# All loop matmuls in 64x64 parts of the array, in two phases of 64 rows into PSUM bank pairs

## The chip, the cores and the metric

The kernel runs on one core of a Trainium2 chip. A core has a matrix engine (TensorE, "PE" in the profile; its weight loads stand apart as "PEld"), two engines that can read the matrix engine's results (VectorE, "DVE", and ScalarE, "ACT"), GpSimd ("POOL") and SyncE ("SP"), which here mostly issue DMAs. Results of matmuls land in PSUM: 8 banks of 128 partitions by 512 fp32 values. The metric is device time in microseconds. The kernel before took 957.39 us, the median of three runs (953.36, 957.39 and 957.76).

A weight load puts up to 128 rows by 128 columns of weights into the array, and a matmul streams N columns of data past them. The array can be used whole (128*128 in the profile's forms), as two halves of 64 rows (64*128), or as four parts of 64 rows by 64 columns (64*64), each of which has weights, data and results of its own. The profile's form `64*64 64x512` is a matmul in one such part with 512 columns of data. Four of them, one in each part, do the work of one whole matmul; this text calls them a foursome.

## The reference

The inputs are u and v (8 batches of 3136 rows by 256), z (8 by 3136 by 64), three weight matrices and a filter. What is computed, per batch:

```python
scores = np.matmul(z, z.transpose(0, 2, 1)) / S        # S = 3136
attn = np.maximum(scores, 0.0) ** 2
x = u * np.matmul(attn, v)
x1, x2, x3 = split(x @ w_proj, 3)                      # 256 columns each
x2_conv = irfft(rfft(x2, axis=1) * rfft(filter, axis=0), n=S, axis=1)
out = (x1 * x2_conv * x3) @ w_out
```

The matrices of the attention are far too large to be stored, so scores are made in pieces, squared, and summed into the product with v at once. The Fourier transforms are matmuls with cosines and sines in two steps (64 by 49), with a trip through DRAM between the steps.

## The kernel before, in words

**Tiling.** The 3136 columns of a batch are cut into 7 chunks (five of 512, one of 256, one of 320: `CHUNKS`, L18), and its rows into 25 tiles of 128 (the last has 64). For each batch and chunk the kernel goes through a list of units of two tiles (four for the chunk of 256).

- **Scores** (letter S, `score_mm`, L1692): a unit's scores go into a PSUM pair, two banks, one for each tile. The contraction is over 64 values only, so the two tiles run in the two halves of the array. ACT or DVE makes R, the positive part (`relu`, L1929, lines L1934 and L1936), and then A, its square (`sq`, L1938, lines L1943 and L1945). Scores are symmetric, so some units aren't computed but taken from an earlier chunk's A by a DMA transpose (tiles `M1`, `M2e`, `M2o`).
- **Weighing** (letters W, w and v, `weigh` L1753 and `weigh_rows` L1736): A times v is summed over all units of the chunk into two accumulators of one bank each, `ps_o0` and `ps_o1` (L577), one for each half of the 256 model columns. A W does this with whole 128*128 matmuls (line L571 in the profile, the helper `matmul`). A w with its later v does the same in halves: first the upper 64 rows into one accumulator and the lower 64 rows into the other, and then, in v, the other way round. [...] This text calls such a change a flip.
- At a chunk's end DVE multiplies the accumulators by u into `xT` (`xe`, L1980, line L1989), which frees them for the next chunk.
- **Projections and first transform** (letters A, and Z in the last batch; `add_proj` L1195, `dft1` L1004): x1, x2 and x3 of the chunk, each in several tasks with one PSUM bank, evicted by ACT or DVE 512 columns at a time (`copy`, L604 and L608), and for x3 by the product with x1 (`gate`, L1231). x2 goes through the first transform and to DRAM (`spec`).
- **Spectrum** (letter Q, `add_quads` L1150): second transform, product with the filter's spectrum (L1323 to L1328), and its inverse. These matmuls run in 64*64 parts and use a PSUM pair, whose banks are evicted by two instructions.
- **End** (letter B, `add_end` L1391): the last transform in matmuls of 128 columns (weights `conv_in`, data `T4`), the gate (L1420), the product with w_out (weights `yT`, data `wo`), and the store.

**PSUM.** Three pairs (`ps_t`, L531) serve S, Q and, bank by bank, A, B and Z; the other two banks are the accumulators.

**What sets the order.** The order of all PE work is a string, `ORDER` (L47): each letter takes the next task of its kind. A second string, `ENGINES`, says of each task that ACT or DVE could do which of them does it. The class `Plan` (L245) walks the string with modelled costs to place everything else in time. In the loop `go` (L381) a change between whole matmuls (A, B, Z, W) and matmuls in halves or parts (S, Q, w, v) is charged 0.096 us, and a flip is held back for `TURN` (0.235 us) after the earlier rows' end:

```python
            if self.mode and half != (self.mode == "S"):
                start += 0.096
...
                elif self.flip not in (None, task.flip):
                    start = max(start, self.turned + TURN)
```

When a stretch of letters S, Q, w, v holds a Q, all its matmuls use 64*64 parts, otherwise 64*128 halves (`plan.quarters`).

Of the kernel before, what the change touches and what calls it, by code (L numbers as in the profile page):

```python
# [11 lines left out]
P = 128  # L12
F32 = mybir.dt.float32
# [5 lines left out]
N1 = 64  # L19
# [16 lines left out]
SPARE = 0.25  # L36
# [3 lines left out]
MOST = 6  # L40
TURN = 0.235
REACH = 2
# [5 lines left out]
    "ASSAWSSAWWSSAWwSwSvvSSwWBWSSvSWWSSSWWWWWWSSSWWWWwwSvSwwvSSvSwwwSvSvvvAAAWWWABABAWWWAWWAWAAAAAAWBSSww"  # L48
    "SvSSvwwwSvvSwvSSvWWBWWBWWWBWWBWAAAAWWSwSSwwwSSvvvSwwSvvvSWAWAWABAWWWBWWWAWSwSSwWWASwSSvvvSSSWWWWAAWB"
    "WWWASSWAAAWWBWAWWASwSSvwSSvSWWWBSSWAAWWAAAWAWBWWBwSwSwSSwwSvvvvvSWBWWWAAWWAWAAAWWSSSWWWwSvSSWAAWSSwS"  # L50
    "wwQQvvvSQSWWWWSSAAWWWAWAAAWWAAAAWSSwSwwSQvwvvQSvwSQwSwSWAAvvQSvSWWWWWSQSWWWWAwSwSvvSwwQSSvwwQvSvwvSS"
    "vWAWAWWAWAWAWAAWWAAWAQQwQwSSwwAAAAQvvQwvvSwSSvwSvQvSWWAWWWSQSWWAWAWWSQwSwwSvwQvSvwQSwQvvSvSWWWWWAAWW"
    "WAWAWWAQSWAAAAWSwSSwQvQvSWWAWWWSSSWAAWAAAWWAWSSwSwwwSvSvvwvSvSSWAWWAAWAAWWSSSWWWWBBAWBWWBWAAWSSSwwSv"
    "vSSWWABBBWWBAAAAAWWBBWWASSAWWWASSBWBAAAWSwSwSvvwSvwSwwSvSSvvWAWBBWBAWWWBAWWBAWAWSSwwSwSSWABABvSvQvwS"
    "SwSvwvSSvQWWWWBWWAWSAWAWAWQQwSwQvwvSwQwSvvvwSSvwQvSWWBBAAAAWSQSWWBBWWAAWAAWWABQQWwSSQvwSwwQvSwQvvSSv"
    "WWAWABWAWWSQSWWAAWWWAAWAAAAAWSSwQwQvSvSWAASWWWWWSSSWWWWwSwwSwSSvwwvSvvSvvSWWWWBWAWWSSWBWWWABBAWBASww"
    "SSvwSvwSSvvSwwBABAWBBASvSvSWWBWAWAABABWWWABAAAWWSwSSWBAWBAvwSwwSSvwSvvSvSWWBABBWAWBAAAWWAAWBWWSSSWWA"
    "AAAABSwSwwSQvvQvwSSwwQvvSvQSWWWWBWWWASQAWWWQSSwwwSWAWvSQwQvvwSSvBWAABAWSSvQWWWSSQWWWAWWwQQwwSwQvvSSv"
    "vwSSWWWWSvSWBAWAWWWWAAWABAAWASwwSQwwSSvvvSQvWWBAWAABWAWWQSSWWWAAWAWwSSSwwwSSvvAAWvSvSSWWWAWWWSSWWAAB"
    "WBBAWABAWBABSwSwSwwSvvSvwwSvwSSvvvSAWWWAABABBBWABWWSSBBWAAAWABWBWAAAWSSwwSwSvwwvvSSvvwSSvABBWWWWSSSW"  # L60
    "WWAAAWBAWAABAWSSQwWBBWBASvSSwwSwSQvwvvQvQSWWWWAWWAAWWBAWABWSQwQwwSwSvvSQSvvwQwQvQvSWAWBWAAAWWWAWAWSS"
    "SWWWAWBQQwwSQvwvSSwSwvwQSvvQvSWWWWWAWAWAAWWAWQwwSSvvSwwSSvSvWWWAWAAAWAWAAAWWWWSSwSvSwwSSvABAAwSvSwwS"
    "vvvSSWAWBWBWBWWBWBWSSAWBWWASSwSvwSSWABWBAAAwSvSSvwwSvSvWBWWABWAWWAAABAAWAAAWSSSWWAWWWBBwSSvwSvwSSSvW"
    "WWWWBAWBASSWAWBBAWWWSwwSwSvvSSvwSwwSvSvvwQvSSWWWWABWAWAAWAWWWWQQSwwQSvwwvQSSvwvwQQvSvWBWWAABAAAABBWW"
    "WSSWAAWWQQSWBWSwwSQwQvSwvSQvwSWAWvvSSWWAWWAWAAWAWWWASwQvwQwSvSwvSSvWAWWAAWWWAAWAWWWSSQwwwSSvwwvSSvQv"
    "vSSBWAWBASSBWWWAAAWAAWWSSSWWWBAWwSSwSWWBASvSvwwSSvwvSSvBWABAWABBBAAAAWAABAWBWWSSSWWABWBWWABSwSSwwwSw"
    "SvvSvvSSvWWBABWSSAWBWBWABWAWAAAWWAAABWSwSwwSvSvvSwwwQSvQvSvwQWWBBvQSAAWBWWWWWAWABAAAAWQwwwSSSvvvQwww"
    "SQvSvwSvSvSWAAWWBWWSSQWWWBAWAWWSQQwwwSwQQvvvSwvSwQvSvSWAWAWAWWBWAWAWSQAWWWAWSSwwQSWvvSQSWWWWBWAWAAWA"
    "AWWSwSSvwSvSwwSvvSSWWWBAAWWAAWWBWWSSSWWBBBAAWBBWSwSvSwwSSvBWABBAWSwSSvvwSvSABWWBWWSSSWWBWABAAWWBBAWA"
    "AABAABWAASwSSvwwSwSvwvSwSvSvvSSWWWWWBWAWAWABWWSSwQwwwSSvvQwvSwvSQvvwQSvQWBWBAWABWWWAAWWAQSWWBAwSwQQv"  # L70
    "wSwQvwwSwSQvvvQvvSQSWWWWAWWAWWBAAWAWSwSwSSvvSwwwSvvSSvSWWWWAWBWAWWQSSWWWWWAWASSwQwQvvSABAWWWBWBWWWWS"
    "QWWSSwwSSvwvSSvWWWZWWWWWWWAZZAAZAAZAZBZZBZBZBZBZBZBZBBZBZZQQQZQQQQQQQQQZQQQQBBZBZZZZZZBZZZZZBZZZBZBZ"
    "BZBZBBZBBBBBBBBBBBBBBBBBBBBBBB"
)
# [2008 lines left out]
```

## Time and profile before

| what | value |
|---|---|
| times of three runs | 953.36, 957.39, 957.76 us |
| span of the profiled execution | 958.1 us |
| PE busy | 923.5 us, 96% of the span, 9264 matmuls |
| weight loads busy | 508.8 us, 53%, 9352 loads |
| DVE busy | 861.3 us, 90% |
| ACT busy | 836.5 us, 87% |
| POOL busy | 198.1 us, 21% |
| mean granted TensorE clock | 0.989 |

The profiled execution has 958.1 us from its first to its last instruction, 0.7 us more than the median of the timed runs, so sums made against its span are carried over to the time by taking off 0.7 us. A line of groups gives engine, operation, result and operands by the program's names, the form (weights' rows * columns, then data's partitions x elements), the count, and after the bar the busy time with the mean duration of one; after the second bar stands the engine's idle time before them. A row of the timeline gives start, length, engine, and how many instructions of one kind are merged in it. A matmul's end is modelled: a matmul of 512 columns is drawn some 380 ns long although the next one starts earlier than that. So the pitch, from start to start, says more than the drawn lengths, and a gap in the issue that is shorter than the drawn tail doesn't show as idle time.

### The profile page before, as it was taken

Reading aid. Unit: us, or ns where it says so; the run is one execution under the profiler, and the core shown is the slowest. Engines: PE = TensorE matmul, PEld = TensorE weight load, DVE = VectorE, ACT = ScalarE, POOL = GpSimd, SP = SyncE. Lnnn points to the kernel's source line nnn. Section 1 sums busy time; section 2 is a strip of 40 time slices with the busy share of each in tenths; the row PEclk is TensorE's granted clock in tenths of the full one; section 3 lists DMA queues with packets and bytes.
Section 4 is the critical chain, followed back from the end, with each engine's and each line's share of the span. In section 5 each row is a group of like instructions: output and inputs, shape, how many; then the busy total and the mean of one; then the engine's idle time right before and its main releaser. Section 6 shows DMA issues by size and latency. Waiting matters only on the chain.

```text
span 958.1 us, 24530 instructions
## 1 busy us (share of the span) xinstructions
PE 923.5 (96%) x9264; PEld 508.8 (53%) x9352; DVE 861.3 (90%) x1508; ACT 836.5 (87%) x1145; POOL 198.1 (21%) x426
## 2 busy tenths in 40 slices
PE   7999899999999999999999999999999999999986
PEld 3444555455455655546555565555555465565654
DVE  8886789898899997999899998899999989999896
ACT  6977699998889998998989989899988999998674
POOL 5132311122112111213031121121211320101031
PEclk8999999999999999999999999999999999999989
DMA  9999889967999789997999979998799989885768
GB/s 147 167 150 171 133 154 186 195 132 152 193 207 194 151 172 178 200 196 146 174 212 203 172 162 177 186 195 167 169 176 210 198 155 194 183 204 126 188 186 264
DMA packets 332423, 170.64 MB, mean 178 GB/s; under 512 B 242598, under 2 KB 307942, under 8 KB 332304
## 3 DMA queue, kind: packets, MB, share of 16 engines
q1 hardware_dynamic: 302424, 132.28, 67.3%
q0 software_dynamic: 29168, 35.13, 24.8%
q10 hardware_dynamic: 712, 1.66, 0.6%
q8 instruction: 73, 1.20, 0.5%
q14 instruction: 46, 0.38, 0.2%
HBM read 90.26 MB, written 53.35 MB: 150 GB/s over the span
## 4 chain that ended last, share of the span: by engine, by line
PE 85%; DMA 6%; DVE 3%; issue 2%; ACT 2%; SPq 2%; POOL 0%; DVEq 0%; ACTq 0%; POOLq 0%
PE ps_s L571 35%; PE ps_o_t L571 27%; PE ps_o_t L1734 23%; DMA spec_in_t<-spec 1%; DMA M_t<-spec_in_t 1%; DMA conv_in_t<-spec 1%; ACT R_t L1934 1%; DMA A_t<-spec 1%; DMA M2e_t<-A_t 1%; DMA spec<-gs_t 0%; DVE xh L1323 0%; DMA M_t<-A_t 0%; SPq L1048 0%; DMA spec<-uT_t 0%; DVE R_t L1936 0%
## 5 line engine op out<-in xcount | busy, mean ns | idle before, releaser
L1934 ACT ACTIVATE R_t<-ps_s 128x1024 f32<-128x1024 f32 (+2 forms) x349 | 325.2, 973 | 34.5 <-PE ps_s L571 29.0
L1943 ACT ACTIVATE A_t<-R_t 128x1024 bf16<-128x1024 f32 (+3 forms) x307 | 304.5, 1018 | 13.7 <-DMA M2e_t<-A_t 6.0
L571 PE MATMUL ps_o_t<-A_t,v_t 128*128 128x512 bf16 (+2 forms) x1080 | 250.2, 352 | 6.0 <-issue 5.1
L1734 PE MATMUL ps_o_t<-A_t,v_t 64*64 64x512 bf16 (+5 forms) x2708 | 228.3, 355 | 0.1
L1945 DVE TENSOR_TENSOR A_t<-R_t 128x1024 bf16<-128x1024 f32 (+4 forms) x185 | 197.3, 1087 | 13.4 <-ACT R_t L1934 11.6
L571 PEld LDWEIGHTS <-v_t 128*128 128x128 bf16 x1534 | 139.5, 98 | 129.6 <-issue 31.9
L1936 DVE TENSOR_SCALAR R_t<-ps_s 128x1024 f32<-128x1024 f32 (+4 forms) x163 | 178.1, 1110 | 23.5 <-PE ps_s L571 13.0
L1734 PEld LDWEIGHTS <-v_t 64*64 64x64 bf16 (+1 forms) x3808 | 134.1, 103 | 106.9 <-PE ps_o_t L1734 21.4
L571 PE MATMUL ps_s<-zT_t 64*64 64x512 bf16 (+4 forms) x1521 | 175.6, 352 | 7.6 <-ACT R_t L1934 4.2
L654 POOL COPY tick<-xT_t 1x1 bf16<-1x1 bf16 x54 | 11.6, 214 | 648.0 <-DVE xT_t L1989 648.0
L571 PE MATMUL ps_s<-xT_t,wp 128*128 128x512 bf16 (+2 forms) x412 | 108.2, 353 | 2.0 <-DVE yT_t L1420 0.4
L604 ACT ACTIVATE x_t<-ps_s 128x512 bf16<-128x512 f32 (+2 forms) x149 | 82.5, 579 | 29.1 <-PE ps_s L571 25.7
L571 PEld LDWEIGHTS <-zT_t 64*64 64x64 bf16 (+1 forms) x1554 | 64.1, 102 | 76.1 <-issue 40.3
L1989 DVE SCALAR_TENSOR_TENSOR xT_t<-ps_o_t,uT_t 128x256 bf16<-128x256 f32 (+2 forms) x224 | 75.8, 380 | 12.6 <-PE ps_o_t L571 9.4
L1231 DVE TENSOR_TENSOR gate_t<-ps_s,x_t 128x256 bf16<-128x256 f32 (+2 forms) x220 | 74.2, 382 | 11.1 <-PE ps_s L571 8.5
L1323 DVE TENSOR_TENSOR xh<-xh,H 128x1024 bf16<-128x1024 bf16 x120 | 81.4, 682 | 0.6
L1734 PE MATMUL ps_o_t<-M_t,v_t 64*64 64x512 bf16 (+2 forms) x808 | 65.6, 364 | 0.0
L1420 DVE TENSOR_TENSOR yT_t<-ps_s,gate_t 128x512 bf16<-128x512 f32 (+2 forms) x99 | 59.0, 618 | 5.6 <-PE ps_s L571 4.6
L645 POOL DMA_DIRECT2D un_t<-in_u_dram x112 | 60.1, 559 | 6.1 <-issue 2.5
L664 POOL DMA_DIRECT2D v_t<-in_v_dram x112 | 59.1, 549 | 10.6 <-issue 6.1
L571 PEld LDWEIGHTS <-wp 128*128 128x128 bf16 x448 | 42.4, 98 | 33.9 <-issue 5.3
L571 PE MATMUL ps_s<-wp,xT_t 128*128 128x256 bf16 x400 | 58.8, 273 | 0.1
(175 smaller groups left out, 1029.2 us busy)
## 6 DMA issues: line engine op xcount, KB each, us to landing
out_dram<-ost_t SPq DMA_DIRECT2D x60, 256.0 KB
spec<-s_t SPq DMA_DIRECT2D x96, 128.0 KB
spec_in_t<-spec SPq DMA_DIRECT2D x56, 192.0 KB
spec<-gs_t SPq DMA_DIRECT2D x56, 192.0 KB
v_t<-in_v_dram POOLq DMA_DIRECT2D x80, 128.0 KB, 5.1
un_t<-in_u_dram POOLq DMA_DIRECT2D x80, 128.0 KB, 5.6
conv_in_t<-spec SPq DMA_DIRECT2D x34, 256.0 KB
out_dram<-ost_t SPq DMA_DIRECT2D x18, 128.0 KB
```

The costliest lines, as they stand in the source:

```text
L571: wrote(nc.tensor.matmul(o, *args, **kw), o)
L604: got = nc.scalar.activation(out_, in_, AF.Copy)
L645: nc.gpsimd.dma_start(out=t[ds(j * N1, N1), lo - t0 : hi - t0, :], in_=x[:, n2 : n2 + hi - lo, :])
L664: nc.gpsimd.dma_start(out=t[ds(j * N1, N1), ds(v_at(a), (b - a) * D)], in_=r[:, n2 + a - lo : n2 + b - lo, :].rearrange("p t d -> p (t d)"),)
L1231: got = nc.vector.tensor_tensor(g[:, ::-1] if h == 0 else g, p, x, ALU.mult)
L1323: nc.vector.tensor_tensor(x[:, 1 - i], x[:, 0], h, ALU.mult)
L1734: row_sums[dh] = h, nc.tensor.matmul(*args, **kw)
L1934: has_read(nc.scalar.activation(r, p, AF.Relu), p)
L1936: has_read(nc.vector.tensor_single_scalar(r, p, 0.0, ALU.max), p)
L1943: nc.scalar.activation(a, r, AF.Square)
L1945: (nc.vector if e == "DVE" else nc.gpsimd).tensor_tensor(a, r, r, ALU.mult)
L1989: nc.vector.scalar_tensor_tensor(x, f, inv_s2, ut, ALU.mult, ALU.mult)
```

## The change

- Every matmul of the loops now runs in 64*64 parts. The form of the array is a property of the task (`full`): only the transposes of the setup (four for z, one for T4, two for TZ) are still whole.
- The letter W is gone. All 648 weighing tasks of the string are now w, each with its v.
- Tasks of A, B and Z are made by `two`: a first phase, in which the upper 64 rows feed bank 0 of a pair and the lower rows bank 1, and a second phase, a letter of its own later in the string, with the rows swapped. Ahead of the second phase PE waits for the first one's last matmul.
- PSUM is four pairs for everything. The accumulators of a chunk are one pair, taken from the four when the chunk's first w starts, and freed by the eviction. A task that used one bank now takes a pair, and what were two evictions of 512 columns is one of 1024 (`dft1`, x1, x2, Q outside the last batch, the gates, `xe`, the end); the tiles in SBUF are joined to fit.
- The square of R now carries the scale 1/S, so that `xe` is a plain product.
- One projection task covers the chunk where x2, the first transform and the output product had one task for each two tiles.
- Both strings are new. `ORDER` has 2637 letters (648 w, 648 v, 512 S, 424 A, 229 B, 136 Q, 40 Z) where it had 2530 (643 W, 285 w, 285 v, 512 S, 408 A, 222 B, 136 Q, 39 Z); `ENGINES` has 1426 (921 for ACT, 505 for DVE) where it had 1746 (1137 and 609).

The core of the diff:

```diff
-MOST = 6
+FORM = 0.096
...
 ORDER = (
-    "ASSAWSSAWWSSAWwSwSvvSSwWBWSSvSWWSSSWWWWWWSSSWWWWwwSvSwwvSSvSwwwSvSvvvAAAWWWABABAWWWAWWAWAAAAAAWBSSww"
+    "ASSASwSAvSwAvSwSvwSwSvvwSwSvSvwSvwSvwSvwSvwBvwSvSwAvAwSwSvwwvSSwwAvvSwvSwwvAvvvwBvBwSwwSSvwAAAAvwvSv"
...
-            if self.mode and half != (self.mode == "S"):
-                start += 0.096
-                self.flip, self.parted = None, True
...
+            if self.full is not None and self.full != task.full:
+                start += FORM
+            self.full = task.full
+            if k in "wv":
+                flip, turned = self.flips.get(task.sum, (0, 0.0))
+                if k == "w":
+                    task.flip = flip
+                    task.second.flip = flip ^ 1
                     self.rest.append(task.second)
-                elif self.flip not in (None, task.flip):
-                    start = max(start, self.turned + TURN)
-                self.flip, self.parted, self.turned = task.flip, False, start + task.cost["PE"]
+                elif flip != task.flip:
+                    start = max(start, turned + TURN)
+                self.flips[task.sum] = task.flip, start + task.cost["PE"]
...
-    ps_t = [ps_p.tile([P, 2, 512], F32, name=f"ps_s{i}") for i in range(3)]
+    ps_t = [ps_p.tile([P, 2, 512], F32, name=f"ps_s{i}") for i in range(4)]
...
-    banks = Banks(3)
-    pair_slots, one_slots, half_slots = Pairs(banks), Singles(banks), Halves(banks)
-    ps_o = [Pool(f"ps_o{dh}", 1, [P, 512], F32, PS) for dh in range(2)]
+    pair_slots = plan.pairs = Pairs(4)
...
+    def two(kind, mm, cost, deps=(), takes=(), **kw):
+        box = {}
+
+        def go(ph):
+            if ph == 0:
+                box["p"] = take_pair()
+            else:
+                rest = nc.tensor.nop()
+                for x in box["last"].values():
+                    tc.add_manual_dep(
+                        rest.ins, x.ins.name, mybir.DependencyInfo(needs, reason.DATA),
+                        reason="the other rows' sum",
+                    )
...
+        a = pe(kind, lambda: go(0), cost, deps, [pair_slots, *takes], **kw)
+        b = pe(kind, lambda: go(1), cost, [(a, TURN - LAT["PE"])], **kw)
+        return a, b, box
+
+    QUARTERS = [(h, c) for h in range(2) for c in range(2)]
...
-            for m in range(0, P, N1 if plan.quarters else P):
-                n = N1 if plan.quarters else P
-                matmul(o[ds(m, n)], zt[h, ds(t * P + m, n)], zt[h, ds(C0[at], cw)], start=True, stop=True)
+            for m in range(0, P, N1):
+                matmul(o[ds(m, N1)], zt[h, ds(t * P + m, N1)], zt[h, ds(C0[at], cw)], start=True, stop=True)
...
+    def weigh(un, flip, ph):
 
         b, c, k = un
         cw = CHUNKS[c]
+        if k == 0 and ph == 0:
+            acc[b, c] = take_pair()
+        todo = [(i, t) for i, t in enumerate(plans[b, c][k][1]) if t < NT - 1]
+        for i, t in todo:
+            for m in range(0, P, N1):
                 for h in range(2):
                     dh, at = h ^ flip, slice(h * N1, (h + 1) * N1)
                     by_rows(
+                        (b, c, dh), h, laid(un, acc[b, c][ds(m, N1), dh, :cw]), row(v16[b], t)[at, ds(dh * P + m, N1)], block(un, i, at),
+                        start=k == 0 and i == 0 and ph == 0, stop=k == len(plans[b, c]) - 1 and ph == 1 and i == todo[-1][0],
                     )
...
-                    nc.scalar.activation(a, r, AF.Square)
+                    nc.scalar.activation(a, r, AF.Square, scale=1.0 / float(S))
                 else:
-                    (nc.vector if e == "DVE" else nc.gpsimd).tensor_tensor(a, r, r, ALU.mult)
+                    nc.vector.scalar_tensor_tensor(a, r, inv_s2, r, ALU.mult, ALU.mult)
...
+                    for h, n in halves(c):
+                        x, f = by_half(xt["t"][:], h, n), by_half(acc[b, c][:], h, n)
+                        ut = uT[b, c][:, 0:n, :, ds(h * N1, N1)].rearrange("p t d j -> p d t j")
+                        has_read(nc.vector.tensor_tensor(x[:, :, ::-1] if h == 0 else x, f, ut, ALU.mult), f)
```

More of the change, by code (lines that the diff above doesn't have):

```diff
@@ L39 @@
 ZP, ZL = 0, 0.0
-MOST = 6
+SPARE = 0.25
 TURN = 0.235
+FORM = 0.096
 REACH = 2
@@ L232, in __init__ @@
         self.clogs = False
-        self.second, self.split, self.flips, self.flip = None, False, False, None
+        self.second, self.flips, self.flip, self.full, self.sum = None, (), 0, False, None
         for d, _ in self.deps:
@@ L1754, in weigh, with add_weigh @@
+    w_first, w_last = {}, {}
+    def add_weigh(un, data, done):
         b, c, k = un
[L1755 to L1770 removed]
```

732 lines of the change are left out of this document (317 added, 415 removed).

## The prediction

> **What bounds the kernel now.** I read the page first: the engines' shares and the chain of waits.
>
> ```profile
> span 958.1 us, 24530 instructions
> PE 923.5 (96%) x9264; PEld 508.8 (53%) x9352; DVE 861.3 (90%) x1508; ACT 836.5 (87%) x1145; POOL 198.1 (21%) x426
> ...
> PE 85%; DMA 6%; DVE 3%; issue 2%; ACT 2%; SPq 2%; POOL 0%; DVEq 0%; ACTq 0%; POOLq 0%
> ```
>
> PE is busy 96% of the span and holds 85% of the chain, with DVE and ACT close behind at 90% and 87%. Next I asked for busy times by stretch, to see whether that holds everywhere.
>
> ```profile
> 100.00:900.00 800.00, 786.66 (x8216) 438.71 (x8294) 734.80 (x1255) 725.83 (x985) 151.10 (x325) 1.00 0.92 177
> 900.00:958.00 58.00, 44.75 (x454) 29.60 (x454) 45.76 (x95) 31.97 (x62) 12.28 (x23) 0.91 0.76 226
> ```
>
> The columns are PE, PEld, DVE, ACT and POOL, then clock, DMA share and GB/s. From 100 to 900 us PE idles 13.3 of 800 us at full clock; only the last 58 us, with 13.2 us idle, are of another kind. So the middle is worth what PE's own instruction stream is worth, and "busy" has to be looked into, since a drawn tail can cover a gap in the issue. Third, then, the timeline of PE alone:
>
> ```profile
> 402.17 0.41 PE L571 MATMUL ps_s<-zT_t 64*64 64x512 bf16 x4
> 402.41 0.39 PE L571 MATMUL ps_s<-xh,TZ 64*64 64x512 bf16 x4
> 402.72 0.61 PE L571 MATMUL ps_s<-wp,xT_t 128*128 128x256 bf16 x4
> 403.17 1.46 PE L571 MATMUL ps_o_t<-M2o_t,v_t 128*128 128x512 bf16 x6
> 404.56 0.41 PE L571 MATMUL ps_s<-spec_in_t,S 49*64 49x512 bf16 x4
> 404.80 0.39 PE L571 MATMUL ps_s<-zT_t 64*64 64x512 bf16 x4
> ```
>
> Six whole matmuls of 512 columns take 1.46 us with a last one drawn 0.38 long: (1.46 - 0.38) / 5 = 0.216 us of pitch. The last one therefore starts at 403.17 + 1.08 = 404.25, and the foursome after it at 404.56, 0.31 later. So the change of form cost 0.31 - 0.216 = 0.094 us, none of it drawn as idle. The second foursome follows 0.24 after the first, another 0.024. Back from parts to whole, 402.41 to 402.72 is again 0.31, a loss of 0.094.
>
> **The change part by part.**
>
> *Changes of form.* In the old string, 252 neighbouring letters lie on different sides of S, Q, w, v against A, B, Z, W, half of them into parts. 126 x (0.094 + 0.024) + 126 x 0.094 = 14.9 + 11.8 = 26.7 us, all on PE, which is the path. Afterwards seven tasks of the setup are whole, at most 14 changes: 14 x 0.1 = 1.4 us. Net -25.3.
>
> *The work itself.* Is a foursome as quick as a whole matmul?
>
> ```profile
> 439.66 0.82 PE L1734 MATMUL ps_o_t<-A_t,v_t 64*64 64x256 bf16 x24
> 440.31 0.48 PE L571 MATMUL ps_s<-zT_t 64*64 64x320 bf16 x8
> 440.60 0.63 PE L1734 MATMUL ps_o_t<-M_t,v_t 64*64 64x256 bf16 x16
> 441.03 0.63 PE L1734 MATMUL ps_o_t<-A_t,v_t 64*64 64x256 bf16 x16
> ```
>
> Six foursomes of 256 columns take 440.31 - 439.66 = 0.65, four take 441.03 - 440.60 = 0.43: 0.108 us each. Four whole ones (402.72 to 403.17, 0.45 us) have 0.11. For 512 columns the row at 409.19 below gives two foursomes in 0.46, with 0.024 of that the start after a change: 0.22, against 0.216. The number of columns to be streamed doesn't change, so this costs nothing, except where nothing in the trace shows it: matmuls of 128 columns (the last transform), which never run in parts.
>
> ```profile
> 475.67 0.61 PE L571 MATMUL ps_s<-T,conv_in_t 128*128 128x128 bf16 x8
> 476.11 0.59 PE L571 MATMUL ps_o_t<-A_t,v_t 128*128 128x512 bf16 x2
> ...
> L1734 PEld LDWEIGHTS <-v_t 64*64 64x64 bf16 x2704 | 83.3, 106 | 50.0 <-PE ps_o_t L1734 9.9 <-issue 2.1 <-PE ps_s L571 1.7
> ...
> L571 PEld LDWEIGHTS <-conv_in_t 128*128 128x128 bf16 x332 | 25.0, 98 | 15.2 <-DMA conv_in_t<-spec 1.9 <-issue 1.0
> ```
>
> Whole, eight start in 0.44, a pitch of 0.055, although a load is drawn 98 ns long: loads overlap matmuls. A load of a part is drawn 106 ns, nearly the same. There are 25 tiles x 2 phases x 8 batches = 400 foursomes. Bounds: 0, if the pitch stays 0.055, and 400 x (0.106 - 0.055) = 20 us, if a matmul must wait for the whole drawn load. A gain is excluded, since the columns set 0.055. I take 0: the whole matmuls with a 98 ns load are the nearest row. [...]
>
> *Flips.* What a flip costs depends on what stands between the two sets of rows.
>
> ```profile
> 409.19 0.63 PE L1734 MATMUL ps_o_t<-A_t,v_t 64*64 64x512 bf16 x8
> 409.65 0.39 PE L571 MATMUL ps_s<-zT_t 64*64 64x512 bf16 x4
> 409.89 0.41 PE L1734 MATMUL ps_o_t<-As_t,v_t 64*64 64x512 bf16 x4
> 410.13 0.39 PE L571 MATMUL ps_s<-xh,TZ 64*64 64x512 bf16 x4
> 410.35 0.39 PE L1734 MATMUL ps_o_t<-A_t,v_t 64*64 64x512 bf16 x4
> ...
> 409.89 0.11 PEld L1734 LDWEIGHTS <-v_t 64*64 64x64 bf16 x4 [0.34 <-PE ps_o_t L1734]
> ```
>
> The first rows' last foursome starts at 409.65 - 0.216 = 409.43; the other rows' loads are let go by it at 409.89, 0.46 later. In between stands one score foursome (0.216). Lost: 409.89 - 409.65 - 0.216 = 0.024, and 0.024 more on the next pitch (409.89 to 410.13): 0.05 us. With nothing in between it is 0.46 - 0.216 + 0.024 = 0.27, with two foursomes or more nothing. Behind the waiting load stands all of PE, and through the scores ACT and DVE.
>
> I followed w and v through the new string, chunk by chunk. It has 269 flips, 14 with nothing between and 59 with one S or Q: 14 x 0.27 + 59 x 0.05 = 6.7 us. The old string has 119, 3 and 59: 3.8 us. Net +2.9.
>
> *Two phases for A, B and Z.* The letters 424 + 229 + 40 less seven whole tasks make 343 pairs. Which task a letter takes the string doesn't say. Bounds: 0 if all are filled; 28 us if the 47 places ahead of the last w or v where A follows A or B follows B are bare flips (47 x 0.27 = 12.7) and each of the other 296 has one foursome between (296 x 0.05 = 14.8). I take the mean of the weighing flips, 6.7 / 269 = 0.025: 343 x 0.025 = +8.6. In the last 58 us PE has idle time to hide flips; but the last chunk's own chain gets two flips and longer evictions, +1.0.
>
> *Evictions.*
>
> ```profile
> L1934 ACT ACTIVATE R_t<-ps_s 128x1024 f32<-128x1024 f32 x283 | 282.6, 1037 | 28.7 <-PE ps_s L571 24.6 <-DVE A_t L1945 1.0 <-DVE gate_t L1231 0.6
> ...
> L604 ACT ACTIVATE x_t<-ps_s 128x512 bf16<-128x512 f32 x125 | 73.3, 606 | 27.1 <-PE ps_s L571 23.8 <-DVE x_t L608 2.8
> ...
> L1989 DVE SCALAR_TENSOR_TENSOR xT_t<-ps_o_t,uT_t 128x256 bf16<-128x256 f32 x160 | 59.7, 415 | 9.7 <-PE ps_o_t L571 7.1 <-DMA uT_t<-un_t 1.9 <-DMA out_dram<-ost_t 0.2
> L1420 DVE TENSOR_TENSOR yT_t<-ps_s,gate_t 128x512 bf16<-128x512 f32 x72 | 47.1, 680 | 4.2 <-PE ps_s L571 4.0
> ```
>
> Two of 512 on ACT are 2 x 0.606 = 1.21, one of 1024 is 1.04; `xe` goes from four of 0.415 (1.66) to two of about 0.68 (1.36). Some 0.15 to 0.3 us are saved each time, on engines that wait for PE (28.7 us before R alone). I credit 0, hidden behind PE; the other bound is the middle's 13.3 us of PE idle, which is all that quicker evictions could give. The scale in the square adds no instruction.
>
> *Four pairs in place of three and two banks.* The next chunk's first w no longer waits for the eviction of the old accumulators. But one-bank tasks hold a pair through two phases, and at each of the 56 chunk ends two accumulators leave two pairs for the rest.
>
> ```profile
> ACT R_t L1934 <- PE ps_s L571: 29.0, 42, 2.3
> ...
> PE ps_s L571 <- ACT R_t L1934: 4.4, 3, 3.1
> ```
>
> Today ACT waits for scores far more (29.0 us) than scores for ACT (4.4). I take 0; below, a gain of those 4.4, above, the rival's 34.
>
> *Sum.* 958.1 - 25.3 + 0 + 2.9 + 8.6 + 1.0 + 0 + 0 = 945.3 us of span; less the 0.7 between this span and the median time of 957.39, **944.6 us**, 1.3% faster. DMA is busy 0.92 of the middle, so its 736 us still fit in the 13 us less that the middle would last.
>
> **The rivals.**
>
> *Flips eat the gain.* If the pairs cost the upper 28 and not 8.6, it is 944.6 + 19.4 = 964; halfway, 954. For it: A next to A at 47 places, and 612 flips where there were 119. Against: `Plan` charges a flip about what the trace shows. I put it at 957, no change.
>
> *PE waits for pairs* (the other side). While an accumulator is evicted, scores and projections share two pairs. A score's pair is held for a drawn matmul of 0.38 and an eviction of 1.04; with a w or v of 0.43 to fill in, PE stands 0.6 us longer, 56 x 0.6 = 34: 979. Past 18 us, 0.32 us for each chunk end, the kernel is slower by over 0.5%. For it: DVE and ACT near 90%, and fewer, larger holds. Against: PE already waits little for ACT, and much weighing can be placed there.
>
> *Loads bound the 128-column foursomes:* 944.6 + 20 = 965, decided at the last transform, where the count and both prices stand above.
>
> *All flips filled and PE's idle halved:* 944.6 - 8.6 - 6.7 = 929, if the quicker evictions do reach PE.
>
> That the change doesn't do what it says is not open: the form follows from the operands' partitions.
>
> **How the numbers follow.** Half a per cent, 4.8 us, is about what a measurement of this kernel can tell from no change: below 952.6 is faster, above 962.2 slower. Chances: the forecast 0.56 (its own range 936 to 952), the better case 0.12, flips 0.14 (0.09 of it within half a per cent, 0.03 faster, 0.02 slower), pairs 0.11, loads 0.07. Faster is 0.56 + 0.12 + 0.03 less 0.03 for the forecast's upper edge = 0.68; same 0.09 + 0.03 = 0.12; slower 0.02 + 0.11 + 0.07 = 0.20. The range from 932 to 966 leaves out most of the pairs' case and part of the better one, some 0.17.
>
> **What would show it.** Right: nearly all matmuls are 64*64, about four times as many, foursomes of 512 keep 0.216 us; from 100 us on each batch ends some 1.5% earlier; loads waiting on PE itself add up to some 10 to 20 us. Wrong: PE idle in the middle well over 13 us with ACT or DVE as releaser of its matmuls (pairs), or foursomes of 128 columns 0.1 us apart (loads). The forecast falls if the middle's 800 us of work don't come out 9 to 20 us shorter.

## The result and the profile after

The changed kernel takes **994.62 us** (median of four runs, 990.99 to 998.33), the kernel before beside it 955.38 us (952.08 to 957.76): a ratio of 1.042, with a 95% interval of 1.038 to 1.047. The forecast was 944.6 us, within 932 to 966; the kernel is slower by 39 us where 13 us less were forecast. Some executions take 1.5% or more longer than the fastest of the same kernel; ratios and intervals below leave them out, medians in us hold all executions unless the text says otherwise.

The page of the kernel after, with the span, the engines' busy times, the chain that ended last, by engine and by line, and two of the DMA queues:

```profile
span 992.8 us, 47200 instructions
PE 926.9 (93%) x21077; PEld 647.7 (65%) x21077; DVE 850.2 (86%) x1128; ACT 817.2 (82%) x933; POOL 196.1 (20%) x426
...
q1 hardware_dynamic: 301624, 131.98, 70.9%
...
q8 instruction: 164, 2.69, 1.2%
...
PE 38%; DMA 8%; DVE 4%; ACT 2%; issue 2%; SPq 1%; DVEq 0%; ACTq 0%
PE ps_s L486 38%; DMA M_t<-A_t 4%; DVE xh L1316 1%; ACT R_t L1869 1%; DVE A_t L1880 1%; DMA spec<-s_t 1%; DVE yT_t L1419 1%; DMA spec<-gs_t 1%; DMA spec_in_t<-spec 1%; DVE R_t L1871 1%; DMA M2e_t<-A_t 1%; ACT A_t L1878 0%; DVE xT_t L1919 0%
```

The span has grown by 34.7 us, and not by PE's work. The shares of the chain add up to 55% here, because it could be followed back only to 438.55 us; of what it covers PE holds some 68% (37.8 of 55), where it held 85% of the whole span before. The transfer that the chain names first is `M_t<-A_t`: the DMA transposes which take squared scores (A_t) of an earlier chunk to the tiles M_t, M2e_t and M2o_t. PE now executes 21077 matmuls; q8, of which more below, stood at this in the page before:

```profile
q8 instruction: 73, 1.20, 0.5%
```

The busy times by stretch, after (PE, PEld, DVE, ACT, POOL, clock, DMA share, GB/s):

```profile
100.00:900.00 800.00, 761.39 (x17395) 535.04 (x17387) 699.36 (x893) 689.28 (x769) 146.66 (x319) 0.99 0.99 174
900.00:992.00 92.00, 72.80 (x2029) 57.06 (x2019) 67.15 (x96) 50.95 (x78) 13.73 (x27) 0.97 0.69 181
```

In the middle, from 100 to 900 us, PE idles 38.6 us, and the DMA share has gone from 0.92 to 0.99, though 174 GB/s are moved and not 177. The profile before showed 13.3 us there, which is too much: its page has 9264 matmuls for 9352 weight loads, so 88 records of matmuls are missing. The same instructions were profiled once more in `before_nops` (below), with all 9352 matmuls:

```profile
PE 932.5 (98%) x9352; PEld 508.7 (53%) x9352; DVE 861.4 (90%) x1508; ACT 836.1 (88%) x1145; POOL 197.9 (21%) x426
```

There PE is busy 795.9 of the 800 us in the middle and idles 4.1. So PE's busy time has fallen, from 932.5 to 926.9 us, and its idle time in the middle has grown from some 4 to 38.6.

The waits of the kernel after (time in all, times, longest):

```profile
DVE A_t L1880 <- DMA M_t<-A_t: 22.8, 10, 4.7
ACT R_t L1869 <- DVE A_t L1880: 20.2, 9, 4.2
PE ps_s L486 <- DVE A_t L1880: 14.4, 6, 4.3
...
ACT A_t L1878 <- DMA M2e_t<-A_t: 10.7, 3, 7.6
...
ACT A_t L1878 <- DMA M_t<-A_t: 7.0, 7, 1.9
...
DVE A_t L1880 <- DMA M2o_t<-A_t: 4.3, 1, 4.3
```

and those of the kernel before on the same tiles:

```profile
ACT A_t L1943 <- DMA M2e_t<-A_t: 6.0, 3, 3.5
...
DVE A_t L1945 <- DMA M_t<-A_t: 0.9, 1, 0.9
ACT A_t L1943 <- DMA M_t<-A_t: 0.7, 2, 0.5
```

DVE and ACT wait 44.8 us for buffers of A_t that a transpose still reads (2.5 more are in a smaller row); before it was 7.6. One such stall, in the timeline of the kernel after (start, length, instructions, and in brackets the idle time and what ended it):

```profile
326.31 3.59 SPq L1468 DMA_DIRECT2D out_dram<-ost_t  x4
330.01 5.07 SPq L1799 DMA_TRANSPOSE M_t<-A_t  x2
335.18 2.31 SPq L1365 DMA_DIRECT2D spec<-gs_t  x3
337.53 2.22 SPq L1799 DMA_TRANSPOSE M_t<-A_t  x1
...
344.38 1.56 DVE L1880 SCALAR_TENSOR_TENSOR A_t<-R_t 128x640 bf16<-128x640 f32 x2 [4.65 <-DMA M_t<-A_t]
345.26 0.72 PE L486 MATMUL ps_s<-A_t,v_t 64*64 64x320 bf16 x8 [4.27 <-DVE A_t L1880]
345.30 0.70 ACT L1869 ACTIVATE R_t<-ps_s 128x640 f32<-128x640 f32 x1 [4.18 <-DVE A_t L1880]
```

Behind four stores SP is held 5.07 us by two transposes, and after three writes of the spectrum 2.22 by a third; DVE wants to write the square into a buffer that a transpose has not left, and stands 4.65 us; ACT and PE behind it stand over 4.

Beside the longest stalls the trace shows a second price, a lower clock. PE's granted clock falls to 0.50 from 345.3 to 348.8 us, just after this one, and in four more stretches of the middle, 20.5 us in all; each begins within 1.1 us of the end of an idle time of PE of 2.0 to 4.3 us. In one of them, from 437.5 to 444.3 us, a foursome of 512 columns takes 0.42 us (439.36 to 439.78), where it takes 0.22 at full clock:

```profile
438.55 1.07 PE L486 MATMUL ps_s<-wp,xT_t 64*64 64x256 bf16 x16 [3.29 <-DVE ost_t L553]
439.36 0.69 PE L486 MATMUL ps_s<-xh,TZ 64*64 64x512 bf16 x4
439.78 1.11 PE L486 MATMUL ps_s<-wp,xT_t 64*64 64x256 bf16 x16
```

The kernel before has 3.4 us at half clock in the middle. By an estimate from these numbers, half of 20.5 less half of 3.4, some 8 of the 39 us are lost that way, on top of the idle time.

### The profile page after: what moved, and what is told of

It reads as the page before. It is cut to its first block, busy times and chain, and to the rows that moved or that the text cites. A ratio compares the mean times of both kernels' runs of the same rounds, so it can differ in the third digit from the quotient of the medians.

```text
span 992.8 us, 47200 instructions
## 1 busy us (share of the span) xinstructions
PE 926.9 (93%) x21077; PEld 647.7 (65%) x21077; DVE 850.2 (86%) x1128; ACT 817.2 (82%) x933; POOL 196.1 (20%) x426
## 2 busy tenths in 40 slices
DMA packets 331708, 171.78 MB, mean 173 GB/s; under 512 B 242887, under 2 KB 307143, under 8 KB 331505
## 3 DMA queue, kind: packets, MB, share of 16 engines
q8 instruction: 164, 2.69, 1.2%
## 4 chain that ended last, share of the span: by engine, by line
PE 38%; DMA 8%; DVE 4%; ACT 2%; issue 2%; SPq 1%; DVEq 0%; ACTq 0%
PE ps_s L486 38%; DMA M_t<-A_t 4%; DVE xh L1316 1%; ACT R_t L1869 1%; DVE A_t L1880 1%; DMA spec<-s_t 1%; DVE yT_t L1419 1%; DMA spec<-gs_t 1%; DMA spec_in_t<-spec 1%; DVE R_t L1871 1%; DMA M2e_t<-A_t 1%; ACT A_t L1878 0%; DVE xT_t L1919 0%; DMA A_t<-spec 0%; DVE R_t L1316 0%
## 5 line engine op out<-in xcount | busy, mean ns | idle before, releaser
L486 PE MATMUL ps_s<-A_t,v_t 64*64 64x512 bf16 (+2 forms) x8096 | 530.2, 354 | 18.8 <-DVE A_t L1880 14.4
L486 PEld LDWEIGHTS <-v_t 64*64 64x64 bf16 x11044 | 357.8, 107 | 167.3 <-issue 30.3
L1869 ACT ACTIVATE R_t<-ps_s 128x1024 f32<-128x1024 f32 (+4 forms) x357 | 330.3, 951 | 69.8 <-PE ps_s L486 46.9
L1878 ACT ACTIVATE A_t<-R_t 128x1024 bf16<-128x1024 f32 (+4 forms) x274 | 266.2, 990 | 28.6 <-DMA M2e_t<-A_t 10.7
L1880 DVE SCALAR_TENSOR_TENSOR A_t<-R_t 128x1024 bf16<-128x1024 f32 (+3 forms) x218 | 239.8, 1120 | 38.0 <-DMA M_t<-A_t 22.8
L486 PE MATMUL ps_s<-zT_t 64*64 64x512 bf16 (+2 forms) x2128 | 199.8, 356 | 6.1 <-ACT xh L549 1.8
L486 PE MATMUL ps_s<-xT_t,wp 64*64 64x512 bf16 (+2 forms) x1792 | 129.4, 355 | 0.8 <-issue 0.7
L486 PEld LDWEIGHTS <-zT_t 64*64 64x64 bf16 x2161 | 83.9, 107 | 45.3 <-issue 11.6
L486 PE MATMUL ps_s<-M_t,v_t 64*64 64x512 bf16 (+2 forms) x1408 | 97.5, 354 | 4.1 <-DMA M_t<-A_t 2.8
L1215 DVE TENSOR_TENSOR gate_t<-ps_s,x_t 128x512 bf16<-128x512 f32 (+2 forms) x112 | 64.5, 618 | 15.6 <-PE ps_s L486 10.3
L486 PE MATMUL ps_s<-wp,xT_t 64*64 64x256 bf16 (+1 forms) x1664 | 69.2, 273 | 3.3 <-DVE ost_t L553 3.3
```

Of the source, the lines that this page charges most:

```text
L486: got = nc.tensor.matmul(o, *args, **kw)
L1215: has_read(nc.vector.tensor_tensor(o[:, :, ::-1] if h == 0 else o, p, x, ALU.mult), p)
L1869: has_read(nc.scalar.activation(r, p, AF.Relu), p)
L1878: nc.scalar.activation(a, r, AF.Square, scale=1.0 / float(S))
L1880: nc.vector.scalar_tensor_tensor(a, r, inv_s2, r, ALU.mult, ALU.mult)
```

## The experiments

Theory 1 was that the transposes are late and block DVE, ACT and PE in turn; theory 2, that pairs of PSUM with less slack let any late transfer through; theory 3, that PE waits for its own flips: where other rows follow into an accumulator or a bank, the kernel makes PE wait for the earlier rows' last matmul. Every version keeps the order of the work of the kernel it is made from. Ratios are to the kernel before, timed beside each version. `xt_7` below differs from the kernel after by one buffer and has a ratio of 1.033 where that had 1.042, so differences of under some 1% between versions timed apart say little.

**Transposes replaced by plain copies, after and before.**

```diff
-                nc.sync.dma_start_transpose(out=o, in_=live[un][:rows, ds(i * cw, len(ts) * cw)])
+                if a == NC - 1:
+                    x = live[un][:, ds(i * cw, n * rows)].rearrange("p (n j) -> p n j", n=n)
+                else:
+                    o, x = m[:, ds(j * cw, len(ts) * cw)], live[un][:, ds(i * cw, len(ts) * cw)]
+                nc.sync.dma_start(out=o, in_=x)
```

> The changed kernel with each DMA transpose of squared scores (A_t into M_t, M2e_t, M2o_t) replaced by a plain copy of as many bytes in the same place of SP's queue, with the same waits; the blocks below the diagonal are left untransposed, all else is done. Theory 1 (transposes that land late hold the squared-score buffers, VectorE and ScalarE wait for them in order, and TensorE runs dry): most of the 46 us of middle stalls goes, 945 to 958 us. Theory 2 (half the slack of the PSUM pairs, so that any late transfer reaches TensorE, the spectrum loads and the stores too): only the stalls that stand behind transposes by name go, 965 to 978 us. Theory 3 (TensorE waits for its own flips of rows and phases): no change beyond 5 us, 988 to 996 us.

> The kernel before with the same replacement (blocks below the diagonal left untransposed). It is the control. Theory 1: its engines waited some 8 us for these transposes against some 45 us after the change, so 947 to 955 us, a gain of at most 9 us. Theories 2 and 3: the same or no change, 950 to 956 us. If it gains as much as the changed kernel does, the transposes cost both the same and theory 1 falls.

After: **945.1 us** (940.41 to 946.46; ratio 0.989, 0.983 to 0.995), a gain of 49.5. Before: **946.8 us** (0.992, 0.989 to 0.995), a gain of 7.3 on the 954.14 beside it. Some 42 of the gain are the changed kernel's own, the whole of its loss. The middle of the changed kernel with copies:

```profile
100.00:900.00 800.00, 790.87 (x18640) 574.64 (x18632) 736.87 (x946) 717.03 (x806) 153.81 (x333) 1.00 0.85 185
```

PE idles 9.1 us of 800, and its granted clock is 1.00. That is theory 1; theory 2 had 965 to 978 us and falls. But it says only where the loss passes, not what makes the transposes late; and since the copies also take the DMA share from 0.99 to 0.85, this run alone doesn't tell the transposes' form from their load on the DMA engines.

**No flips.** The row-to-bank assignment is kept in both phases, so that nothing waits for other rows.

```diff
+                todo = [(c, bank ^ ph, *x) for c, bank, *x in todo]
...
-        t = pe("W", lambda: weigh(un, t.flip, 0), cost, deps, [pair_slots] if k == 0 else [])
-        t.second = Task(lambda e: weigh(un, t.flip ^ 1, 1), {"PE": cost}, [(t, ISSUED)])
+        t = pe("W", lambda: weigh(un, 0, 0), cost, deps, [pair_slots] if k == 0 else [])
+        t.second = Task(lambda e: weigh(un, 0, 1), {"PE": cost}, [(t, ISSUED)])
```

> The changed kernel in which the upper rows always sum into the first bank and the lower rows into the second, in both phases and in every weighing, so that no rows ever follow others into a bank and no wait for that is left (only the 64-row remainders keep it); it leaves out the crossed half of the products and adds the others twice, with the same number and shapes of matmuls in the same order. Theory 3: 955 us or less. Theories 1 and 2: the flips that the trace shows cost 28 us of weight loads' waiting, much of it beside other work, and a faster TensorE only comes sooner to the same late transfers: 980 to 992 us.

Four runs took 977.53, 992.99, 997.12 and 1001.71 us, median **995.05**, too far apart for a ratio. None comes near the 955 us of theory 3, which falls. But the fastest is 17 us below the median of the kernel after, so that flips take no part at all isn't shown.

**Stores on another queue.** `by=nc.gpsimd` in the stores of the first six batches.

> The changed kernel with the output stores of the first six batches issued by GpSimd rather than SP, at the same place of the order. Theory 1 in the form that the transposes come late because they stand behind the stores in SP's queue: 970 to 985 us. Theory 1 in the form that they come late because their target tile is still read by the weighing matmuls: 989 to 999 us. Theory 2: 985 to 995 us. GpSimd's own issue cost could make it slower, to 1000 us.

Three executions took 986.74 to 989.24 us, median **988.41** (1.035, 1.030 to 1.041); the fourth, which was profiled, took 5405 us, and its profile is not used. The 6 us less say little (`xt_7`, with the stores where they were, has 1.033), and the same edit brings nothing in the halves below (`halves_a9_pool`). That the transposes stand behind the stores is not what makes them late.

**The target tile never read.** Weighing takes its data from a constant tile.

```diff
-        m, nb = mirrors[b, a, c], pair[i] - tiles[a][0]
...
+        x = wp16[:].rearrange("p k n -> p (k n)")[at, 0:cw]
+        return x if c == NC - 1 else x.rearrange("p (i j) -> p i j", j=P)
```

> The changed kernel with all its DMA transposes, but the weighing of the blocks below the diagonal reads a constant tile (the projection weights) instead of M_t, M2e_t and M2o_t; so no transpose waits for matmuls that still read its target, and no matmul waits for a transpose. It leaves out the use of the transposed blocks. The runs before it have shown that the transposes carry the loss (945.1 us with plain copies). Theory 1a (they start late because their one target tile is still read by the two-phase weighing): 945 to 960 us. Theory 1b (they are slow themselves: SyncE's issue of each is blocked and their packets take long beside the other DMA): 975 to 992 us.

**1003.3 us** (1.049, 1.044 to 1.055), above the ranges of both forms; why it is slower than the kernel after stays open. No transpose waits for PE any more (in the kernel after SP waited 78.9 us for PE ahead of them), yet the waits for them are there nearly as before. The waits of this kernel:

```profile
DVE A_t L1878 <- DMA M_t<-A_t: 15.6, 7, 4.1
...
ACT A_t L1876 <- DMA M2e_t<-A_t: 8.4, 3, 5.6
...
ACT A_t L1876 <- DMA M2o_t<-A_t: 5.4, 2, 3.1
```

So theory 1a falls: the transposes themselves are slow. SP's records agree: its 260 transposes hold it 400.7 us in the kernel before and 446.0 after, for nearly the same bytes; the 172 of A_t among them, 272.2 and 298.9.

**More buffers.** The pool of A_t gets 9 or 10 buffers, that of xT_t 7 or 6.

> Control for the next two: the changed kernel with 7 buffers of xT_t instead of 8 and everything issued in the same order. All theories: 990 to 1002 us, as xT_t is not named among the long waits; if it is slower, the next two are compared with this one.

> 7 buffers of xT_t, and 9 instead of 8 of A_t, same order. If VectorE and ScalarE stop because all squared-score buffers are held by late transposes, one buffer more lets them run about 1.6 us further (one score unit): 15 to 25 us of the 45 us of such waits go, 968 to 985 us. If the stalls begin elsewhere (PSUM pairs, loads), 988 to 1002 us.

> 6 buffers of xT_t, 10 of A_t, same order. Buffers held by late transposes: most of it goes, 955 to 975 us, unless the sixth xT_t buffer is missed. Otherwise 988 to 1005 us.

Control **987.28 us** (1.033, 1.026 to 1.039) without one execution of 1016.45, nine **980.82** (1.024, 1.020 to 1.028), ten **984.57** (1.029, 1.024 to 1.034). The ninth buffer brings 6 to 8 us: its time lies in the range, but the gain is less than the 15 to 25 expected, and the intervals touch. The tenth, with one xT_t less, brings none more, and misses its range of 955 to 975.

**What slows the transposes?** I counted packets in the traces. The packets of 256 bytes on q1 carry the transposes (with plain copies for those of A_t the packets under 512 bytes fall from 242887 to 112070 after the change, and from 242598 to 111782 before it). They have the same median in both kernels (18 ns), but before 1510 of them took over 0.3 us and after 1993; their time, shared by 16 DMA engines, is 86.9 us and 137.1 us. Of the 1993, 874 (44%) begin within 1.1 us after the start of a packet of q8; by chance it would be 164 x 1.1 / 993 = 18%. Before it is 477 (32%), by chance 8%. Those behind a q8 packet make up 40.6 of the 86.9 us and 78.1 of the 137.1: most of the difference. The sums differ by some 15 us from profile to profile (101.9 us in `before_nops`, 152.6 in `xt_7`). SP's records point the same way: a transpose of A_t with the start of a q8 packet between 1.0 us before and 1.2 us after its own holds SP 2.08 us in the mean after (71 of 172) and 1.84 before (45 of 172), the others 1.50 and 1.49. And q8, which the page calls "instruction", follows PE's instructions: its 2.69 MB over 21077 matmuls and as many loads are 64 bytes for each, and the 1.20 MB of the kernel before over 9264 and 9352 are 64 as well. Its packets are all of 16384 bytes in both traces, so one stands for 256 such instructions; below it is called a fetch. That made theory 4, that PE's instruction fetches stop the transposes; its rival, theory 5, is that the fetches have no part, and the new order with its thinner slack is the cause.

**Empty instructions in the kernel before.**

```diff
+    def pad(x):
+        for _ in range(5 if x.shape[0] == P else 1):
+            nc.tensor.nop()
...
```

> The kernel before with empty instructions put behind TensorE's matmuls (5 behind one that contracts 128 rows, 1 behind one of 64), some 23000 of them, so that TensorE's instruction stream is about as long as after the change; nothing else differs. Theory 4: TensorE's instructions come through the DMA engines in 16 KB pieces (queue q8: 73 packets before, 164 after); a piece that meets a DMA transpose stops it for over 1 us on all 16 engines, and the change, which more than doubles TensorE's instructions, doubles the meetings. Then q8 shows about 160 packets, SyncE's transposes take 430 us or more in place of 401, and the kernel takes 975 to 1000 us. Rival theory 5 (the transposes are late because of the changed order of the work and the thinner slack alone, and the instruction stream has no part in it): 950 to 962 us with 160 packets.

**955.78 us** (1.001, 0.998 to 1.005). But q8 still shows 73 packets: the empty instructions never reached the chip, and this run says only that the kernel before repeats, now with a profile that lacks no matmul.

**Half of each foursome left out.** Of the two matmuls that share rows and data, the second is left out, but at a sum's start and end.

```diff
+            todo = [x for i, x in enumerate(todo) if not x[0] or x[5] or x[6] or ph == 1 and last[x[1], x[0]] == i]
...
```

> The changed kernel with only the first 64 of 128 output rows computed in the two-phase products and the weighing, but for the matmuls that open and close a sum: two of the four matmuls of most foursomes are left out, so half of the sums' rows are incomplete. The two that are left stream as many columns through the same parts, so TensorE's time should stay (216 ns for 512 columns), with some 40% fewer instructions and q8 packets near 95. Theory 4: 945 to 965 us. Theory 5: 985 to 1000 us.

**962.12 us** (1.006, 1.003 to 1.009), with 107 packets on q8.

**Two halves in place of four parts.** The two matmuls that share rows, data and bank become one with 128 columns of weights; nothing is left out.

```diff
-            for m in range(0, P, N1):
-                matmul(o[ds(m, N1)], zt[h, ds(t * P + m, N1)], zt[h, ds(C0[at], cw)], start=True, stop=True)
+            p = N1 if QUARTERED[plan.at - 1] else P
+            for m in range(0, P, p):
+                matmul(o[ds(m, p)], zt[h, ds(t * P + m, p)], zt[h, ds(C0[at], cw)], start=True, stop=True)
...
```

> The changed kernel, nothing left out, but with two 64x128 parts instead of four 64x64 ones wherever no DFT matmul is within 20 letters of the order (1800 of the 2637 letters): each pair of matmuls that share rows, moving data and bank becomes one with 128 output rows. TensorE's instructions fall by about a third (q8 near 110 packets); 38 changes of form come in, at 0.09 to 0.12 us. Theory 4: 950 to 970 us, in proportion to the fetches left. Theory 5: 985 to 1002 us. If 64x128 parts do not run side by side at 0.216 us for 512 columns, slower than 1010 us.

**965.64 us** (1.008, 1.005 to 1.012). Instructions and q8 of this kernel:

```profile
PE 919.6 (96%) x13774; PEld 571.9 (60%) x13774; DVE 849.2 (89%) x1128; ACT 816.2 (85%) x933; POOL 196.1 (20%) x426
...
q8 instruction: 108, 1.77, 0.8%
```

The same products in the same order, with a third fewer instructions, give back 29.0 of the 39 us. Two versions with as many fetches, one of them with work left out, agree within some 4 us. Theory 5 by itself falls, since the order is the same. That PE's streaming isn't what changed is seen in its timeline:

```profile
349.71 0.38 PE L498 MATMUL ps_s<-A_t,v_t 64*128 64x512 bf16 x2
349.93 0.39 PE L498 MATMUL ps_s<-zT_t 64*128 64x512 bf16 x2
350.15 0.61 PE L498 MATMUL ps_s<-A_t,v_t 64*128 64x512 bf16 x4
350.60 0.38 PE L498 MATMUL ps_s<-xT_t,wp 64*128 64x256 bf16 x4
```

A pair of halves takes 0.22 us for 512 columns, as a foursome does. SP is held 425.9 us by its transposes, between 400.7 and 446.0.

**More fetches in the kernel before.**

```diff
-        wrote(nc.tensor.matmul(o, *args, **kw), o)
+        whole = args[0].shape[0] == P and size(o) == 512
+        for k in range(2 if whole else 1):
...
+            wrote(nc.tensor.matmul(part[0], args[0], part[1], **how), part[0])
...
```

> The kernel before, nothing left out, same order, but its 64x128 parts are made of two 64x64 ones and its matmuls of 512 columns are cut into two of 256 with the same weights: as many columns stream, by some 8000 more matmuls and weight loads. (The empty instructions tried first never reached the chip: q8 stayed at 73 packets.) TensorE's work should take about as long (256 columns at 108 to 109 ns, 512 at 216), q8 should show 125 to 140 packets. Theory 4 (instruction fetches stop the DMA transposes): about 0.5 us for each further fetch, as between the changed kernel (164 fetches, 994.6 us) and its halves (108, 965.6 us): 975 to 990 us, with SyncE's transposes up from 401 to 420 us or more. Theory 5 (order and slack alone): 950 to 962 us. If TensorE itself is slower at the shorter matmuls, the gaps inside the foursomes show it and the price is taken off.

**1003.01 us** (1.049, 1.045 to 1.053), with 138 packets. The size is more than theory 4 gave, and the way is another: SP's transposes take 408.9 us, hardly more, and DVE and ACT wait 8.5 us for them. Yet the long packets are as many as after the change (1931, 145.7 us, of which 103.6 behind a q8 packet). So fetches beside transposes are not enough for the waits on A_t: in the old kernel they hardly arise. Here it is PE that stands, and not for a semaphore. Its timeline:

```profile
743.78 0.61 PE L1755 MATMUL ps_o_t<-A_t,v_t 64*64 64x256 bf16 x16
744.22 0.39 PE L586 MATMUL ps_s<-zT_t 64*64 64x256 bf16 x6
747.36 0.42 PE L586 MATMUL ps_s<-zT_t 64*64 64x256 bf16 x2 [2.76 <-issue]
747.36 2.12 PE L1755 MATMUL ps_o_t<-A_t,v_t 64*64 64x256 bf16 x32
```

A foursome breaks off after two of its four matmuls and goes on 3 us later. "Issue" means that the profile shows nothing it waited for; by the packet records, a q8 packet had landed 1.46 us earlier. Of the 13 idle times of over 1 us in the middle of this run 12 end 1.2 to 1.55 us after one; eleven of these have no wait in them at all, and add up to 22.1 us. PE had run out of instructions, as these times suggest. Half clock adds to it (17.1 us in the middle, against 3.4 before). The rest would be the shorter matmuls' work (two of 256 columns take 218 ns, one of 512 takes 216) and smaller gaps, which were not added up.

**The split matmuls with copies.** Both edits on the kernel before.

> The kernel before with the shorter matmuls (138 fetches) and with plain copies for the transposes of squared scores (blocks below the diagonal untransposed). In before_split TensorE stood 13 times for 1.3 to 3.3 us and began again 1.2 to 1.55 us after a 16 KB fetch had landed, with no semaphore to wait for. Theory 4 in its full form (fetches and transposes hold each other up, both ways): without those transposes the fetches come in time, 952 to 965 us, that is the 946.8 us of the kernel before with copies and some 8 us for the shorter matmuls (two of 256 columns take 218 ns, one of 512 takes 216). If fetches are late whatever else runs: 980 to 1000 us.

**979.21 us** (1.023, 1.020 to 1.027): a gain of 24, but 32 more than `before_copy`. So 32 of the split's 48 us stay without the transposes, and the time lies just under the 980 to 1000 of fetches that are late whatever else runs. The full form of theory 4 doesn't hold; in this kernel PE seems to outrun its fetches. With copies it still stands five times over 1 us in the middle without a semaphore, 10.3 us in all, against eleven times and 22.1. By an estimate from the pitches, a foursome of 256 columns uses 8 instructions in 109 ns, so the 256 of a fetch (16384 bytes at 64) last 3.5 us; with 512 columns they last 6.9.

**The halves with copies.**

> The halves with plain copies for the transposes of squared scores (blocks below the diagonal untransposed). Theory 4: fetches only cost where transposes stand beside them, so this comes to the 945.1 us of the changed kernel with copies, 940 to 950 us, though it has 56 fetches fewer and 38 form changes more. If fetches cost TensorE directly, it is faster than that by 15 us or more.

**934.76 us** (0.979, 0.974 to 0.984), 10.3 below `after_copy`: under the 940 to 950 of theory 4, and short of the 15 us or more of fetches that cost TensorE directly. So 56 fetches more cost some 10 us without those transposes and 29 with them, in this order; the 38 changes of form that the halves add are not taken off.

**Halves with more buffers and stores elsewhere.**

> The halves with 9 buffers of A_t and 7 of xT_t. With 8 and 8 the change from 164 to 108 fetches brought 29 us; the ninth buffer brought 10 us at 164 fetches. If both act on the same waits: 955 to 962 us; if they add: 953 to 957 us.

> The same with the output stores of the first six batches issued by GpSimd, which brought 6 us at 164 fetches: 948 to 958 us, perhaps faster than the kernel before (955.5 us).

> The halves with 9 buffers of A_t and 7 of xT_t, and with 64x64 parts only within 10 letters of DFT matmuls instead of 20: some 11 fetches fewer (near 97), 52 form changes more at 0.1 us. By the 0.5 us for a fetch the two cancel: 952 to 960 us, as halves_a9 (956.2 us).

**956.17 us** (1.001, 0.997 to 1.004), **959.79** (1.005, 1.002 to 1.008) and **953.39** (0.9966, 0.9936 to 0.9996). The second, with the stores on GpSimd, is above its 948 to 958; the others lie in their ranges. With 97 fetches the last is the one version without work left out whose interval lies below both kernels, by a third of a per cent; as the best of several it is best called equal to the kernel before. Its page:

```profile
PE 922.5 (97%) x12416; PEld 547.6 (58%) x12416; DVE 849.5 (89%) x1128; ACT 818.4 (86%) x933; POOL 196.6 (21%) x426
...
q8 instruction: 97, 1.59, 0.7%
```

## Why the prediction was wrong, point by point

*Changes of form, work and flips: the way is borne out, the size not measured apart.* Foursomes of 512 columns keep their pitch (408.12, 408.55 and 408.99 below, two in each row: 0.22), and those of 128 columns too: four are drawn in 0.39 with a last one of 0.22, so (0.39 - 0.22) / 3 = 0.057 us.

```profile
408.12 0.60 PE L486 MATMUL ps_s<-M2o_t,v_t 64*64 64x512 bf16 x8
408.55 0.60 PE L486 MATMUL ps_s<-A_t,v_t 64*64 64x512 bf16 x8
408.99 0.60 PE L486 MATMUL ps_s<-M2o_t,v_t 64*64 64x512 bf16 x8
...
509.87 0.39 PE L486 MATMUL ps_s<-T,conv_in_t 64*64 64x128 bf16 x16
```

The loads rival is dead: its sign was foursomes of 128 columns 0.1 us apart. A load of 64 columns is drawn 107 ns here and one of 128 columns 98 ns in the kernel before, but that did not make this transform slower (0.057 us against the 0.055 of its whole matmuls). Loads wait 27.9 us for PE itself, more than the 10 to 20 of the forecast; but the kernel before has 24.3 of this, so it was a poor sign, and no run of `no_flip` came near the 955 us that would make flips the loss. What form changes and flips bring together is seen best with copies, where all matmuls are in both profiles and the clock stays at 1.00 in the middle:

```profile
PE 928.6 (98%) x9352; PEld 508.0 (54%) x9352; DVE 861.0 (91%) x1508; ACT 835.9 (88%) x1145; POOL 198.7 (21%) x426
PE 912.2 (97%) x21077; PEld 652.5 (69%) x21077; DVE 848.0 (90%) x1128; ACT 816.0 (87%) x933; POOL 196.6 (21%) x426
```

PE's busy time falls by 16.4 us from `before_copy` to `after_copy`, but the time by only 1.7. `halves_copy` is 12.0 us faster than `before_copy`, and the sum gave 12.8: an agreement that is in part luck, since the halves also have 35 fetches and 38 changes of form more.

*Pairs: not the cause.* The forecast's sign for this rival did appear, PE idle in the middle well over 13 us with DVE and ACT as releasers. (The 13.3 us, here and as the bound of the evictions, was itself misread: with all records it is 4.1.) Yet with the same four pairs and the same order `after_copy` idles 9.1 us there. The sign was badly chosen: an engine that releases matmuls can itself be stopped by a DMA, as DVE was here for 22.8 us by `M_t<-A_t`, and it is the wait ahead of it that tells.

*Evictions at 0:* not tested apart.

*The step that failed is in the sum:* "DMA is busy 0.92 of the middle, so its 736 us still fit". It counted the data's transfers as given, and it had no term for PE's instructions, though the text itself forecast "about four times as many" matmuls. In its place the runs showed that a third fewer instructions give back 29.0 of the 39 us, and copies for the transposes all of it. The page counts the fetches among the packets of the same 16 DMA engines. They are few (1.2% of the engines' time), so the price isn't their own time: by SP's records a transpose of A_t near a fetch takes longer (2.08 us against 1.50), as the packet counts say too, and a late transpose holds A_t, then DVE, ACT and PE (4.65, 4.18 and 4.27 us in the stall at 345 us). None of the rivals named it.

*How much is shown.* That the loss passes through the transposes is shown by the copies (42 us, all of it). That fewer instructions alone give back 29 of the 39 is shown by the halves; some 10 of these come back without the transposes too, by `halves_copy`. That PE stands until a fetch has landed is read from `before_split` (12 of 13 idle times); in the changed kernel itself a few stalls look the same, such as this one, which ends 1.53 us after a fetch had landed:

```profile
802.14 0.60 PE L486 MATMUL ps_s<-xT_t,wp 64*64 64x512 bf16 x6
803.42 0.40 PE L486 MATMUL ps_s<-xT_t,wp 64*64 64x512 bf16 x2 [0.68 <-issue]
```

That a fetch stops a transpose is argued, not shown: it rests on the counts of packets, the holds of SP and the halves; no run changed the fetches alone without touching PE's matmuls, since the empty instructions fell away. `before_split` shows that more fetches alone don't bring the waits on A_t about: something else of the change is needed, and the new order with its thinner slack is the likeliest, since a ninth buffer helps. How the last 10 us, which the halves don't give back, divide between their 35 fetches more than before and the thinner slack of the new order stays open; with nine buffers of A_t the halves come to the time of the kernel before (956.17 us, ratio 1.001).

## What to carry to other kernels

Count the instructions of a change, not only its columns and bytes: in these traces 256 of them, matmuls and loads, went with one 16 KB fetch on q8, and a fetch cost 0.2 us without the transposes of A_t (10.3 / 56) and 0.5 us where they stood beside it with few buffers (29.0 / 56). That is no fixed price: in the kernel with shorter matmuls 65 fetches more cost 32 us even without those transposes, 0.5 us each, its other costs included. Where parts of the array share rows, data and bank, one matmul with wider weights did the same here at the same pitch (0.22 us for 512 columns) for half the instructions. When an engine is named as the releaser of a stall, ask for that engine's own wait before blaming it, and test the transfer by putting a cheaper one in its place with the same waits. Compare the counts of matmuls and weight loads in a page before reading its idle time.

## What the runs showed of the hardware that was not expected

- The 256-byte packets of DMA transposes take 18 ns in the median, but some 1% take 0.3 to 3 us, many at a time (up to 26 under way at once in the kernel after), and 44% of these there begin within 1.1 us after the start of a fetch on q8, where chance would give 18%.
- In `before_split` PE went on 1.2 to 1.55 us after a fetch had landed, in 12 of 13 idle times over 1 us, one of them in the middle of a foursome.
- An idle time of PE of 2.0 to 4.3 us was followed or met by 3.4 to 6.8 us at a granted clock of 0.50, five times in the middle of the kernel after.
- Pairs of 64*128 halves keep 0.22 us for 512 columns; by the starts in the trace of the halves, a change from halves to 64*64 parts takes 0.31 us where the pitch is 0.22, a loss of 0.09, as between whole and parts; the way back takes 0.32 to 0.37.
